# Attention in visits on four 64x64 tiles of TensorE, with a re-timed emission and another load order

## The chip, the cores and the metric

The kernel runs on one core of a Trainium2 chip. Its engines are TensorE (PE; its weight loads are shown apart as PEld), VectorE (DVE), ScalarE (ACT), GpSimd (POOL) and SyncE (SP). The metric is the device time of one execution in microseconds (us); the kernel before has a median of 285.37 us over three runs (285.2 to 285.39).

## The reference

Eight batches of eight heads, 576 positions, head size 64. Retention in parallel form, then a feed-forward with exact GELU:

```python
scores = scale * np.matmul(q, k.transpose(0, 1, 3, 2))
gamma = 1.0 - 2.0 ** (-5.0 - np.arange(H, dtype=np.float32))
Dmat = np.where(rel >= 0, gamma[:, None, None] ** rel[None, :, :], 0.0)   # rel = pos[:, None] - pos[None, :]
attn = np.matmul(scores * Dmat[None, :, :, :], v)
x = attn.transpose(0, 2, 1, 3).reshape(B * S, H * D)      # 4608 x 512
h = x @ w_in                                              # 512 x 2048
g = 0.5 * h * (1.0 + erf(h * inv_sqrt2))
out = g @ w_out                                           # 2048 x 512
```

## The kernel before

**Attention.** The 576 positions are cut into chunks of 128 with a tail of 64, and two batches are worked on together as a pair. A unit is one chunk of one batch (indices 0 to 35; a tail unit holds the tails of both batches of a pair). For a pair of units four things stand on PE: `scores` (k against q, line 535, `sc`), `inner` (values against the masked scores, line 600, `o_ps`), `state` (the decayed sum of k times v that the next chunk reads, line 619, `u_ps`), and `cross` (the state of the chunks before against q, line 653, into the same `o_ps`; a first chunk has none). VectorE masks the scores (`ret`, line 558) and takes `o_ps` out into the rows of x (`xT`); the values are scaled per head into `vh`, in one instruction on DVE or in eight on ACT. The scores of one pair are emitted beside the inner products of the pair ahead of it, so the step that stands together on PE is: inner, state, scores, cross, with small differences of order.

How these use the array of 128 by 128: `inner` and `state` contract over 128 rows and write 64 partitions of the result, so two halves of the columns work side by side. `scores` and `cross` contract over 64 rows and write 64 partitions, so four quarters work side by side. The feed-forward uses the whole array.

**Feed-forward.** Nine blocks of 512 rows of x. `hT` (line 701) is x times w_in, `g` its GELU on ACT, and `oT` (block 0) or seven products with sums of blocks (`m`, line 885; a Strassen form in 2 by 2) give the output. From block 6 the first product is in that form too (`f`, line 966).

**What sets the order.** The program is written by an emission loop that keeps a clock for each engine, with costs and due times written in the code, and at each step emits what its clocks call ready; attention has the first right, then the feed-forward. PE costs are the first argument of `pe(...)`, costs on other engines that of `on(...)`. The table `ORDER` first lists the loads on the POOL queue in order (`wi3` is columns 768 to 1023 of w_in, `k1` the keys of unit 1, `io` the constants, `wo0` rows 0 to 255 of w_out, `dq2` a step of the decay table), then settings: `a7` scales the values of unit 7 on ACT, `s`, `b`, `z`, `p` and `u` delay single steps. In the first 16 us of its clock the loop fills PE's gaps with products of zeros (`warm`). Eight PSUM banks are shared by all products, one bank a result.

```python
if nB < nA:                      # pairs whose scores are there and whose inner products are due
    ...
    cand(max(scored, free_time(n) - 0.3), "S", g, back)
...
elif kind == "S":
    g, back = a
    for i in back:
        inner(i)
```

## Time and profile before

| what | value |
|---|---|
| median of three runs | 285.37 us |
| span of the profiled execution | 283.7 us |
| PE busy | 278.0 us (98%) |
| DVE, ACT, POOL busy | 199.7, 158.8, 114.0 us |
| matrix products on PE | 3361 |

The profile is one execution. A row of the timeline gives the start of a stretch of equal instructions, the time to the end of the last of them, the engine, the line, what is written and read, the shape and the count; a bracket gives idle time ahead of it and what ended it. The products are pipelined, so the time that a stretch really takes is the distance from its start to the start of the next one.

### The profile page before, as it was taken

Reading aid. Unit: us, or ns where it says so; the run is one execution under the profiler, and the core shown is the slowest. Engines: PE = TensorE matmul, PEld = TensorE weight load, DVE = VectorE, ACT = ScalarE, POOL = GpSimd, SP = SyncE. Lnnn points to the kernel's source line nnn. Section 1 sums busy time; section 2 is a strip of 40 time slices with the busy share of each in tenths; the row PEclk is TensorE's granted clock in tenths of the full one; section 3 lists DMA queues with packets and bytes.
Section 4 is the critical chain, followed back from the end, with each engine's and each line's share of the span. In section 5 each row is a group of like instructions: output and inputs, shape, how many; then the busy total and the mean of one; then the engine's idle time right before and its main releaser. Section 6 shows DMA issues by size and latency. Waiting matters only on the chain.

```text
span 283.7 us, 8075 instructions
## 1 busy us (share of the span) xinstructions
PE 278.0 (98%) x3361; PEld 207.6 (73%) x3361; DVE 199.7 (70%) x412; ACT 158.8 (56%) x362; POOL 114.0 (40%) x143
## 2 busy tenths in 40 slices
PE   8989999999999999999999999999999999999994
PEld 3577666688874588548855778558888888888894
DVE  5753483979865595898178867889669968966822
ACT  5676724755456635693298874564565374665320
POOL 8979987993364465625468552000000000000000
PEclk9999999999999999999999999999999999999999
DMA  9999999999999999999999999910003000400133
GB/s 150 165 182 173 188 180 163 146 142 147 172 161 195 190 147 128 156 229 149 135 197 203 147 137 150 222 21 2 0 2 128 23 2 0 151 0 2 74 114 111
DMA packets 152804, 35.39 MB, mean 125 GB/s; under 512 B 141120, under 2 KB 148928, under 8 KB 152768
## 3 DMA queue, kind: packets, MB, share of 16 engines
q0 software_dynamic: 116832, 18.10, 95.3%
q1 hardware_dynamic: 34528, 16.26, 32.9%
q10 hardware_dynamic: 1408, 0.52, 0.7%
q8 instruction: 26, 0.43, 0.7%
q14 instruction: 10, 0.08, 0.1%
HBM read 36.70 MB, written 9.44 MB: 163 GB/s over the span
## 4 chain that ended last, share of the span: by engine, by line
PE 92%; POOL 3%; DMA 3%; issue 0%; DVE 0%; POOLq 0%
PE m L885 35%; PE hT L701 29%; PE f L966 13%; PE oT L746 5%; PE o_ps L600 3%; PE sc L535 3%; DMA w_in<-in_moe_w_in_dram 3%; POOL qk L318 2%; PE o_ps L653 1%; PE u_ps L619 1%; PE qk_ps L482 1%; POOL v_ld L318 1%; POOL w_in L291 1%; PE sc L525 0%; PE o_ps L591 0%
## 5 line engine op out<-in xcount | busy, mean ns | idle before, releaser
L701 PE MATMUL hT<-xT,w_in 128*128 128x512 bf16 (+3 forms) x560 | 87.4, 312 | 0.8 <-DMA w_in<-in_moe_w_in_dram 0.8
L710 ACT ACTIVATE g<-hT 128x512 bf16<-128x512 f32 (+2 forms) x106 | 57.7, 556 | 36.9 <-PE hT L701 36.1
L701 PEld LDWEIGHTS <-w_in 128*128 128x128 bf16 x560 | 48.4, 98 | 33.8 <-DMA w_in<-in_moe_w_in_dram 1.0
L885 PEld LDWEIGHTS <-gs 128*128 128x128 bf16 x656 | 62.2, 98 | 7.7
L885 PE MATMUL m<-w_sum,gs 128*128 128x256 bf16 (+1 forms) x400 | 47.7, 268 | 0.0
L318 POOL DMA_DIRECT2D v_ld<-in_v_dram x40 | 34.0, 854 | 19.3 <-DMA qk_ld<-in_k_dram 8.8
L318 POOL DMA_DIRECT2D qk_ld<-in_k_dram x36 | 30.4, 851 | 21.7 <-DMA qk_ld<-in_q_dram 19.1
L558 DVE TENSOR_TENSOR ret<-sc,msk 128x512 bf16<-128x512 f32 x48 | 30.2, 683 | 12.2 <-PE sc L535 12.2
L318 POOL DMA_DIRECT2D qk_ld<-in_q_dram x36 | 30.4, 851 | 16.9 <-DMA qkT<-qk_ld 6.5
L885 PE MATMUL m<-w_out,gs 128*128 128x256 bf16 x256 | 32.5, 273 | 0.0
L885 PE MATMUL m<-w_sum,g 128*128 128x256 bf16 x256 | 30.9, 273 | 0.0
L572 ACT ACTIVATE vh<-v_ld,dv 128x64 bf16<-128x64 bf16 x120 | 30.0, 339 | 0.0
L782 DVE TENSOR_TENSOR gs<-g 128x1024 bf16<-128x1024 bf16 x32 | 21.8, 686 | 9.0 <-ACT g L710 8.2
L885 PEld LDWEIGHTS <-g 128*128 128x128 bf16 x256 | 24.9, 98 | 3.9
L991 ACT ACTIVATE g<-f 128x512 bf16<-128x512 f32 x36 | 20.2, 590 | 8.9 <-PE f L966 7.5
L786 DVE TENSOR_TENSOR gs<-g 128x1024 bf16<-128x1024 bf16 x32 | 21.6, 684 | 0.0
L672 DVE TENSOR_TENSOR xT<-o_ps,dqT 128x512 bf16<-128x512 f32 (+1 forms) x32 | 18.4, 617 | 4.5 <-PE o_ps L653 4.4
L966 PEld LDWEIGHTS <-w_in 128*128 128x128 bf16 x192 | 18.8, 98 | 2.2
L461 ACT CAST u_sb<-u_ps 128x512 bf16<-128x512 f32 x15 | 8.7, 587 | 16.0 <-PE u_ps L619 16.0
L461 ACT COPY o<-m 128x512 f32<-128x512 f32 x14 | 8.2, 587 | 15.7 <-PE m L885 15.7
L987 ACT ACTIVATE g<-p 128x512 bf16<-128x512 f32 x12 | 7.6, 630 | 14.1 <-DVE p L985 14.1
L966 PEld LDWEIGHTS <-wi 128*128 128x128 bf16 x144 | 14.0, 98 | 1.6
(96 smaller groups left out, 337.6 us busy)
## 6 DMA issues: line engine op xcount, KB each, us to landing
out_dram<-o SPq DMA_DIRECT2D x27, 256.0 KB, 6.3
v_ld<-in_v_dram POOLq DMA_DIRECT2D x32, 128.0 KB, 9.1
qk_ld<-in_k_dram POOLq DMA_DIRECT2D x28, 128.0 KB, 10.7
qk_ld<-in_q_dram POOLq DMA_DIRECT2D x28, 128.0 KB, 8.6
w_in<-in_moe_w_in_dram POOLq DMA_DIRECT2D x8, 256.0 KB, 7.3
w_out<-in_moe_w_out_dram POOLq DMA_DIRECT2D x8, 256.0 KB, 8.0
out_dram<-o SPq DMA_DIRECT2D x14, 128.0 KB, 2.1
qk_ld<-in_q_dram POOLq DMA_DIRECT2D x8, 64.0 KB, 11.4
```

Of the source, the lines that this page charges most:

```text
L318: nc.gpsimd.dma_start(dst, src[2 * bp + jj, :, ci * C:ci * C + n, :].rearrange("h s d -> s h d"))
L461: nc.scalar.copy(dst, src)
L558: nc.vector.tensor_tensor(r, t, by, op=ALU.mult)
L572: nc.scalar.activation(vh[:, h, :], loaded[i][1][:, h, :], AF.Copy, scale=dv[:, h, ci:ci + 1])
L672: nc.vector.tensor_tensor(x_of(i)[:, :, n * x:n * x + n], o, dqT[:, :, ci * C:ci * C + n], op=ALU.mult)
L701: nc.tensor.matmul(hT[:, m, :], lhsT=w[:, cc, o:o + 128], rhs=x_tiles[t][:, cc, lo:hi], start=(cc == 0), stop=(cc == N_DM - 1))
L710: nc.scalar.activation(g_of(t, m0 // 2)[:, m0 % 2:m0 % 2 + n, lo:hi], hT, AF.Gelu)
L782: nc.vector.tensor_tensor(s.rearrange("p m a b -> p m (a b)"), g[:, :, 0, :], g[:, :, 1, :], op=ALU.add)
L786: nc.vector.tensor_tensor(s, g[:, :, :, LEFT], g[:, :, :, RIGHT], op=MINUS)
L885: nc.tensor.matmul(m[:, 0 if apart else ts, :], lhsT=a, rhs=w[:, c0:c1], start=p in begins and mm == 0 and ts == 0, stop=mm == N_DF // 2 - ...
L966: nc.tensor.matmul(m[:, y, :], lhsT=a[:, c], rhs=d[:, c], start=p in (P1, P7) and y == 0 and c == 0, stop=c == 1, skip_group_check=True)
L991: nc.scalar.activation(g[:, :, rows, cols], m, AF.Gelu)
```

## The change

There are three parts.

1. A new function `visit` emits inner, state, scores and cross of a pair as one piece on four 64x64 tiles. Products that contracted over 128 rows are cut into two halves of 64 rows, one on each half of the array's rows, so inner and state have 32 products in place of 16. Of a pair the visit has 32 inner, 32 state, 32 scores and, but for a first chunk, 16 cross. The list has three parts; the second half of each sum over rows stands in the last, behind a wait of PE on a product of its own from the start of the middle part. `whole` says where a visit is taken: when the next pair's scores and all inputs are there by the emission's clock.
2. Costs in the emission are replaced by others (`sum_w` 1.26 for 1.05, the eight scalings on ACT 2.7 for 2.0, products of the tail 0.15 for 0.23, state 0.24 for 0.26, cross 0.2 or 0.12 for 0.23).
3. `ORDER` is another table: among the loads, k, q and v of units 0 to 2 stand ahead of all but two tiles of w_in, and the settings differ. Two units' values are scaled on ACT (`a6`, `a17`) in place of fifteen.

```diff
--- before.py
+++ after.py
@@ -76,6 +76,7 @@
     AHEAD = 14
     A_TURNS = 2
     HOT = 5.3
+    BOTH = 1.1
     N_WARM = 10
     HOLD = 9
 
@@ -193,7 +194,7 @@
         nc.vector.tensor_tensor(s[:, 1], b12, b22, op=MINUS)
         nc.vector.tensor_tensor(s[:, 2], b21, b11, op=MINUS)
         nc.vector.tensor_tensor(s[:, 3:5], w[:, :, 0:256], w[:, :, 256:512], op=ALU.add)
-        ws_at[i] = on("dve", 1.05, land_out[i]) + SEM
+        ws_at[i] = on("dve", 1.26, land_out[i]) + SEM
 
     SW_LATE, HW_LATE = 4.2, 2.8
     TURN_SHARES, STORE_SHARES = (0.455, 0.545), (0.455, 0.545)
@@ -327,15 +328,14 @@
             land[what, i] = (4.6, 5.2)[n] + 0.75 * x
             t = tiles_of(i)
             cast_due[what, i] = (t[1] if what == "v" else t[0][:, "qk".index(what)], first[what, i])
-    ORDER = ("wi1 k1 wi0 io q1 v0 q2 k2 v1 wi2 v2 k3 wi3 q3 v3 wi4 wi5 wi6 k4 q5 k5 q4 v5 wi7 wo1 wo0 k6 v4 dq2 "
...
+    ORDER = ("k1 wi1 io q1 k2 wi0 q2 v0 k3 v1 q3 v2 wi2 wi3 v3 k4 wi4 wi5 q5 dq2 k5 q4 wi7 wi6 v4 wo0 wo1 v6 v5 "
...
 
     BY_ACT = {int(x[1:]) for x in ORDER if x[0] == "a"}
     S_LATE = {int(x[1:].split("+")[0]): float(x.split("+")[1]) for x in ORDER if x[0] == "s"}
@@ -570,7 +570,7 @@
         if by_act:
             for h in range(H):
                 nc.scalar.activation(vh[:, h, :], loaded[i][1][:, h, :], AF.Copy, scale=dv[:, h, ci:ci + 1])
-            st[i]["V"] = on("act", 2.0, at) + SEM
+            st[i]["V"] = on("act", 2.7, at) + SEM
         else:
             nc.vector.tensor_tensor(vh, loaded[i][1], dv[:, :, ci:ci + 1].to_broadcast([128, H, D]), op=ALU.mult)
             st[i]["V"] = on("dve", 0.685, at) + SEM
@@ -590,7 +590,7 @@
                     sl, e = slice(64 * jj, 64 * jj + 64), 64 * (h % 2)
                     nc.tensor.matmul(s["o"][jj][1][e:e + 64, h // 2, :], lhsT=s["vh"][sl, h, :], rhs=s["ret"][0][sl, h, :],
                                      start=(h < 2), stop=False, skip_group_check=True)
-            s["B"] = pe(0.23, 2 * H, "quad")
+            s["B"] = pe(0.15, 2 * H, "quad")
         else:
             s["o"] = [bank([128, HP, 128], FP32, "o_ps")]
             o = s["o"][0][1]
@@ -606,6 +606,99 @@
         elif j == 1 and ci < NCI - 1 and (bp, ci) != (1, 0):
             u_due.append((bp, ci))
 
+    HALF = [slice(0, 64), slice(64, 128)]
+
+    def weave(lists):
+        at, last = [0] * len(lists), None
+        while any(lists):
+            x = min((x for x in range(len(lists)) if lists[x]), key=lambda x: at[x])
+            cols, fn, a = lists[x].pop(0)
+            at[x] += cols
+            last = fn(*a)
+        return last
+
+    def whole(g, back):
+        if len(g) != 2 or len(back) != 2 or back[0] < 4 or units[back[0]][2] != 0:
+            return False
+        bp, ci, _ = units[back[0]]
+        if (bp, ci) == (1, 0) or back != pair_of.get((bp, ci)) or nX != back[0]:
+            return False
+        if ci and u_ready.get((bp, ci - 1), 1e9) > T["pe"] + 0.3:
+            return False
+        if bp and ci == 1 and nX <= units.index((bp - 1, NCI - 1, None)):
+            return False
+        return max(max(st[i].get("V", 1e9), st[i]["R"]) for i in back) <= T["pe"] + 0.3
+
+    def visit(n, bp, ci):
+        pair, g = pair_of[bp, ci], groups[n]
+        if ci == 0:
+            u_bank[bp] = bank([128, H, D], FP32, "u_ps")
+        u_ps, qkT = u_bank[bp][1], sg[n]["qkT"]
+        qT = sg[group_of[pair[0]]]["qkT"]
+        u = u_of(bp, ci - 1) if ci else None
+        at = max(st[i][x] for i in pair for x in "RV")
+        pe_waits(max(at, sg[n]["T"], u_ready[bp, ci - 1] if ci else 0.0))
+        for i in pair:
+            st[i]["o"] = [bank([128, HP, 128], FP32, "o_ps")]
+        got = [[bank([128, HP, 128], FP32, "sc") for _ in range(2)] for _ in g]
+
+        def inner_mm(j, r, e, hp, first):
+            s = st[pair[j]]
+            vals = loaded[pair[j]][1] if pair[j] in raw else s["vh"]
+            return nc.tensor.matmul(s["o"][0][1][HALF[e], hp, :], lhsT=vals[HALF[r], 2 * hp + e, :],
+                                    rhs=s["ret"][e][HALF[r], hp, :], start=first, stop=(not first and hp == HP - 1),
+                                    skip_group_check=True)
+
+        def cross_mm(j, e, hp):
+            return nc.tensor.matmul(st[pair[j]]["o"][0][1][HALF[e], hp, :], lhsT=u[HALF[j], 2 * hp + e, :],
+                                    rhs=qT[HALF[j], 0, 2 * hp + e, :], start=False, stop=False, skip_group_check=True)
+
+        def state_mm(j, r, h):
+            return nc.tensor.matmul(u_ps[HALF[j], h, :], lhsT=loaded[pair[j]][0][HALF[r], 1, h, j, :],
+                                    rhs=st[pair[j]]["vh"][HALF[r], h, :], start=(ci == 0 and h == 0 and j == r), stop=(h == H - 1),
+                                    skip_group_check=True)
+
+        def score_mm(j, c, h):
+            return nc.tensor.matmul(got[j][h % 2][1][HALF[c], h // 2, :], lhsT=qkT[HALF[j], 1, h, HALF[c]],
+                                    rhs=qkT[HALF[j], 0, h, :], start=(h < 2), stop=True, skip_group_check=True)
+
+        tiles = [(r, c) for r in range(2) for c in range(2)]
+        parts = [[[] for _ in tiles] for _ in range(3)]
+        for x, (r, c) in enumerate(tiles):
+            one, mid, two = (part[x] for part in parts)
+            one += [(128, inner_mm, (r, r, c, hp, hp == 0)) for hp in range(HP)]
+            two += [(128, inner_mm, (1 - r, r, c, hp, False)) for hp in range(HP)]
+            (one if r == c else two).extend((64, state_mm, (c, r, h)) for h in range(H))
+            if ci:
+                one += [(128, cross_mm, (r, c, hp)) for hp in range(HP)]
+            (two if r == c else one).extend((128, score_mm, (r, c, h)) for h in (range(4, 8) if r == c else range(4)))
+            mid += [(128, score_mm, (r, c, h)) for h in (range(4) if r == c else range(4, 8))]
+        weave(parts[0])
+        _, fn, a = parts[1][0].pop(0)
+        end = fn(*a)
+        weave(parts[1])
+        tc.add_manual_dep(nc.tensor.nop().ins, end.ins.name,
+                          mybir.DependencyInfo(mybir.DependencyClass.Sync, mybir.DependencyReason.DATA), reason="row tiles")
+        weave(parts[2])
+        done = pe(BOTH + (0.23 if ci else 0.0), 12 * H + 2 * H * (ci > 0), "quad")
+        nonlocal nA, nB, nX
+        nA, nB, nX = nA + 2, nB + 2, nX + 2
+        for j, i in enumerate(g):
+            st[i]["sc"] = got[j], done
+        for i in pair:
+            st[i]["B"], st[i]["Bdone"] = done, True
+        u_ready[bp, ci] = either(0.68, done, u_of(bp, ci), u_ps) + SEM
+        if ci == NCI - 2:
+            release(u_bank[bp][0], u_ready[bp, ci])
+        for i in pair:
+            s_done.add(i)
+        if next_load[0] < len(groups):
+            reload()
+        masked(g[0])
+        for i in pair:
+            evacuate(i)
+        masked(g[1])
+
     def state(bp, ci):
         pair = pair_of[bp, ci]
         assert (bp, ci) == (1, 0) or nX > (pair_of[bp, ci - 1] if ci else pair_of[bp - 1, NCI - 2] if bp else [-1])[-1]
@@ -618,7 +711,7 @@
                 keys = loaded[i][0][:, 1, h, :] if i < 4 else loaded[i][0][:, 1, h, j, :]
                 nc.tensor.matmul(u_ps[64 * j:64 * j + 64, h, :], lhsT=keys, rhs=st[i]["vh"][:, h, :],
                                  start=(ci == 0 and h == 0), stop=(h == H - 1), skip_group_check=True)
-        done = pe(0.26, 2 * H, "col")
+        done = pe(0.24, 2 * H, "col")
         u_ready[bp, ci] = either(0.68, done, u_of(bp, ci), u_ps) + SEM
         u_due.remove((bp, ci))
         if ci == NCI - 2:
@@ -652,7 +745,7 @@
                     sl = slice(64 * j, 64 * j + 64)
                     nc.tensor.matmul(o[64 * e:64 * e + 64, hp, :], lhsT=u[sl, 2 * hp + e, :], rhs=qT[sl, 0, 2 * hp + e, cols],
                                      start=False, stop=(hp == HP - 1), skip_group_check=True)
-        done = pe(0.23, 2 * H, "quad")
+        done = pe(0.2 if j0 is not None else 0.12, 2 * H, "quad")
         for i in g:
             st[i]["B"] = done
 
@@ -1263,6 +1356,11 @@
                 state(*a)
             elif kind == "S":
                 g, back = a
+                if whole(g, back):
+                    visit(group_of[g[0]], *units[back[0]][:2])
+                    while u_due and state_at(*u_due[0]) <= T["pe"] + 0.3 * (nA >= 8):
+                        state(*u_due[0])
+                    continue
                 for i in back:
                     inner(i)
                     nB += 1
```

How it moves the work, at three places. First the POOL queue at the program's start, before and after (`qk_134`, `qk_162`, `qk_225` before and `qk_132`, `qk_148`, `qk_185` after are q and k of units 1, 2 and 3; `w_in_...` one of the eight tiles of w_in, in the order of issue; unit 0's q and k come on other queues):

```order
L291 DMA w_in_132<-in_moe_w_in_dram 128x4x256
L318 DMA qk_134<-in_k_dram 128x8x64
L291 DMA w_in_137<-in_moe_w_in_dram 128x4x256
L143 ISA
L143 IOTA val 128x128
L145 IOTA pos 128x5
L318 DMA qk_134<-in_q_dram 128x8x64
L318 DMA v_ld<-in_v_dram 128x8x64
L318 DMA qk_162<-in_q_dram 128x8x64
L318 DMA qk_162<-in_k_dram 128x8x64
L318 DMA v_ld<-in_v_dram 128x8x64
L291 DMA w_in_196<-in_moe_w_in_dram 128x4x256
```

There the first values (`v_ld`) are the fifth load and the third tile of w_in the ninth. After the change the same queue, from its third load on:

```order
L319 DMA qk_132<-in_q_dram 128x8x64
L319 DMA qk_148<-in_k_dram 128x8x64
L292 DMA w_in_162<-in_moe_w_in_dram 128x4x256
L319 DMA qk_148<-in_q_dram 128x8x64
L319 DMA v_ld<-in_v_dram 128x8x64
L319 DMA qk_185<-in_k_dram 128x8x64
L319 DMA v_ld<-in_v_dram 128x8x64
L319 DMA qk_185<-in_q_dram 128x8x64
L319 DMA v_ld<-in_v_dram 128x8x64
L292 DMA w_in_255<-in_moe_w_in_dram 128x4x256
L292 DMA w_in_265<-in_moe_w_in_dram 128x4x256
L319 DMA v_ld<-in_v_dram 128x8x64
```

Ahead of this piece stand only k of unit 1, one tile of w_in and the constants. The first values move from the fifth load to the seventh, the third tile of w_in from the ninth to the twelfth, and the fourth to the place right behind it.

Second, PE inside a visit, the middle part's end and the last part's start (each product is a weight load and a matmul; `vh` are scaled values, `ret_...` masked scores):

```order
L662 LDWEIGHTS qkT
L662 MATMUL sc<-qkT 64x128
L662 LDWEIGHTS qkT
L662 MATMUL sc<-qkT 64x128
L648 LDWEIGHTS vh [waits PE_49]
L648 MATMUL o_ps<-ret_1790,vh 64x128
L648 LDWEIGHTS vh
L648 MATMUL o_ps<-ret_1792,vh 64x128
```

The last row of scores of the middle part is followed by the second halves of the inner products. Before, on PE too, a pair's inner products stand as one stretch, and the state follows them:

```order
L600 LDWEIGHTS vh
L600 MATMUL o_ps<-ret_2880,vh 64x128
L600 LDWEIGHTS vh
L600 MATMUL o_ps<-ret_2882,vh 64x128
L619 LDWEIGHTS qk_ld [waits DMASW0_49]
L619 MATMUL u_ps<-vh,qk_ld 64x64
L619 LDWEIGHTS qk_ld [waits DMASW1_49]
L619 MATMUL u_ps<-vh,qk_ld 64x64
```

So the scores of the next pair now stand between two halves of the inner products, and the weight load that opens the last part waits for PE itself.

Third, the whole list of PE: a visit is taken seven times, five times with cross and twice at a first chunk, all of them behind the first products on the line of `m` and ahead of the first on that of `f`; the other pairs keep their old form.

2 lines of the change are left out of this document (1 added, 1 removed), and 13 rows, old and new, of the table ORDER.

## The prediction

> **What bounds the kernel now.** I read the page's busy shares and chain first, then PE's waits, then busy time by stage.
>
> ```profile
> PE 278.0 (98%) x3361; PEld 207.6 (73%) x3361; DVE 199.7 (70%) x412; ACT 158.8 (56%) x362; POOL 114.0 (40%) x143
> PE 92%; POOL 3%; DMA 3%; issue 0%; DVE 0%; POOLq 0%
> PE warm L1187 <- DVE zeros L118: 1.2, 1, 1.2
> PE hT L701 <- DMA w_in<-in_moe_w_in_dram: 0.8, 1, 0.8
> 0.00:18.50 18.50, 16.53 (x170) 9.36 (x171) 11.72 (x42) 12.30 (x33) 16.50 (x25) 1.00 1.70 162
> 33.00:75.00 42.00, 42.00 (x581) 30.50 (x580) 33.50 (x79) 21.90 (x51) 32.01 (x40) 1.00 2.08 161
> 75.00:192.00 117.00, 117.00 (x1519) 78.33 (x1518) 85.55 (x167) 72.28 (x182) 52.57 (x64) 1.00 1.79 159
> 192.00:263.00 71.00, 71.00 (x728) 63.09 (x727) 55.51 (x98) 39.13 (x71) 0.00 (x0) 1.00 0.09 31
> ```
>
> The stage rows give length, then busy time of PE, PEld, DVE, ACT and POOL. PE is the bound in the plain sense: the chain is PE for 92%, and PE's whole list of waits has two entries, both in the first 19 us. From 33 to 263 us it is never empty. So nothing can be gained there by ending a wait; the time falls only if PE's own stretches get shorter, or if the start holds fewer warm-up products and waits. It rises if a wait appears where none is now.
>
> **The step that the visit replaces.** These are a step with cross, a first chunk's step, and two pieces that show single rates.
>
> ```profile
> 150.55 0.64 PE L600 MATMUL o_ps<-ret,vh 128*64 128x128 bf16 x16
> 151.02 0.42 PE L619 MATMUL u_ps<-vh,qk_ld 128*64 128x64 bf16 x16
> 151.37 0.64 PE L535 MATMUL sc<-qkT 64*64 64x128 bf16 x32
> 151.84 0.39 PE L653 MATMUL o_ps<-qkT,u_sb 64*64 64x128 bf16 x16
> 152.16 1.04 PE L701 MATMUL hT<-xT,w_in 128*128 128x512 bf16 x4
> ...
> 118.70 0.64 PE L600 MATMUL o_ps<-ret,v_ld 128*64 128x128 bf16 x16
> 119.52 0.64 PE L535 MATMUL sc<-qkT 64*64 64x128 bf16 x32
> 120.09 1.25 PE L701 MATMUL hT<-xT,w_in 128*128 128x512 bf16 x5
> ...
> 110.41 0.32 PE L591 MATMUL o_ps<-ret,vh 64*64 64x64 bf16 x16
> 110.56 0.62 PE L535 MATMUL sc<-qkT 64*64 64x128 bf16 x32
> 111.01 0.29 PE L653 MATMUL o_ps<-qkT,u_sb 64*64 64x64 bf16 x16
> 111.23 0.94 PE L885 MATMUL m<-w_sum,gs 128*128 128x256 bf16 x7
> ```
>
> By distance of starts, the step with cross takes 152.16 - 150.55 = 1.61 us, and the first chunk's 120.09 - 118.70 = 1.39. The same 32 scores take 0.57 when the whole array follows them (119.52 to 120.09) and 0.47 when cross follows (151.37 to 151.84): a change of the array's form costs 0.10. A step before has three such changes: into the halves, from halves to quarters, and back to the whole. A visit has two. The one into it is paid ahead of the first start in both forms, so I leave it out.
>
> On quarters, a product of 128 columns takes between (0.32 - 0.10)/16 = 13.8 ns (cross, 151.84 to 152.16, less the change) and 0.45/32 = 14.1 ns (scores, 110.56 to 111.01). One of 64 columns takes between (0.22 - 0.10)/16 = 7.5 ns (111.01 to 111.23) and 0.15/16 = 9.4 ns (110.41 to 110.56).
>
> A visit with cross has 32 + 32 + 16 = 80 products of 128 columns and 32 of 64. That is 80 x 13.8 + 32 x 7.5 = 1.34 us, or at the upper rates 80 x 14.1 + 32 x 9.4 = 1.43. So the doubled number of products is nearly free: each keeps a quarter of the array busy, where one of the old form kept half. I take 1.34, because a visit is one stretch and the upper rates are of stretches that start anew.
>
> **The new wait inside a visit.** The last part's first weight load waits for a product of PE itself. No row shows PE waiting for PE at close quarters. The nearest rows are a mask that follows scores, and the weight load of a quarter.
>
> ```profile
> 21.24 0.40 PE L516 MATMUL sc<-qkT 64*128 64x128 bf16 x8
> 21.57 2.73 PE L701 MATMUL hT<-xT,w_in 128*128 128x128 bf16 x21
> 21.67 1.29 DVE L558 TENSOR_TENSOR ret<-sc,near 128x512 bf16<-128x512 f32 x2 [1.13 <-PE sc L516]
> L591 PEld LDWEIGHTS <-vh x64: 102/108/110, 73.4 to 225.4; 64*64 64x64 bf16 x64
> ```
>
> Eight scores stand 0.041 us apart. The first mask reads the bank of the seventh, which starts at 21.49, and the mask starts at 21.67: 0.18 from a product's start to whoever waits for it. With the weight load behind it, 0.11, the next product could start 0.29 after the product waited for. Behind that one stand fifteen more scores, 15 x 13.8 = 0.21. What shows is 0.08; the bounds are 0 (the weight load overlaps) and 0.29 (the cover fails). What is queued behind this wait is all of PE, so whatever shows is lost in full.
>
> A visit is then 1.34 + 0.08 + 0.10 = 1.52 against 1.61. A first chunk's has 64 products of 128 columns: 0.88 + 0.24 + 0.18 = 1.30 against 1.39. Both save 0.09, over seven visits 0.63. The ends: 0.17 a visit saved with no wait (1.2 in all); 1.43 + 0.29 + 0.10 = 1.82, 0.21 lost a visit (1.5 in all).
>
> Outside visits the products are the same, but for hT cut into fewer pieces, whose columns are the same. Counting changes of form along both lists from the first oT on gives 53 against 61: seven belong to the visits, one is left: 0.10 saved.
>
> **The values scaled on DVE.** Thirteen units move from ACT to DVE.
>
> ```profile
> L572 ACT ACTIVATE vh<-v_ld,dv x120: 332/337/372, 13.8 to 172.2; 128x64 bf16<-128x64 bf16 x120
> L575 DVE TENSOR_TENSOR vh<-v_ld,dv x21: 680/682/1052, 14.0 to 224.2; 128x512 bf16<-128x512 bf16 x21
> ```
>
> DVE gets 13 x 0.68 = 8.9 us, ACT loses 13 x 8 x 0.337 = 35. I cost this at nothing, because between 75 and 192 us DVE is busy for 85.55 of 117 and has 31 us free. With no cover, a visit would wait one such instruction, 0.68. The other new costs only change what the emission believes; what they do is in the orders already counted.
>
> **The start.**
>
> ```profile
> L1180 PE MATMUL warm<-zeros 128*128 128x512 bf16 x23 | 6.0, 382 | 0.0
> 17.07 0.62 PE L701 MATMUL hT<-xT,w_in 128*128 128x128 bf16 x8
> 18.47 1.05 PE L701 MATMUL hT<-xT,w_in 128*128 128x256 bf16 x8 [0.78 <-DMA w_in<-in_moe_w_in_dram]
> ...
> 11.04 7.39 DMA w_in<-in_moe_w_in_dram
> 1.25 0.88 POOL w_in L291
> ```
>
> In both orders the same products stand ahead of the first oT, so the start differs by warm-ups and waits alone. Before, 23 warm-ups (behind the first ten) are 23 x 0.22 = 5.1 us, and 18.47 - 17.07 less 8 x 0.056 of work is 0.95 of waiting (the row's bracket counts 0.78 of it, the rest lies in modelled ends): 6.0. After, 22 warm-ups are 4.8. The values of unit 0 now come two loads later, 2 x 0.88 = 1.8 us at the queue's pace, and the first hT with them; that is what the warm-ups cover. Behind them the list is work without warm-ups that needs v1, q3, v2 and the third tile of w_in in turn, each about as early as it lands. That tile is issued about 1.25 + 11 x 0.86 + 0.36 for the constants = 11.1 us, when the fourth was before, the one that needed 7.39 us. It would be there at 18.4 if it is hit in the same way, and PE, some 0.3 us later than before at this place, would wait 0.6. I take 0.9 for all waits of the start together: 4.8 + 0.9 = 5.7, 0.3 saved. The ends are no wait (1.2 saved) and 2.1 us of waits (0.9 lost): the hit of 1.4 on a load that PE stands waiting for, and 0.7 for v1 to v2.
>
> **The sum.** 0.63 + 0.10 + 0.3 = 1.0 us off 283.7, a span of 282.7. The profiled execution's span lies 1.7 under the median of 285.37, so I forecast 284.4.
>
> **The rivals.**
>
> *Nothing to measure.* The visit's wait shows in full or the upper rates hold, and the start gains nothing: a visit at 1.61, only the 0.10 is left, 285.3. For it: no row has a PE wait of this kind. Against: the fifteen scores are there as cover.
>
> *The start gets worse.* The whole 0.9 is lost at v0 to w_in: 285.37 - 0.73 + 0.9 = 285.5, still within the measurement. Against: loads of equal size have gone out by the fourth tile in both orders.
>
> *Slower: banks after a visit.* Before, scores end ahead of cross and DVE may begin on them; a visit's results all end with it.
>
> ```profile
> 151.36 0.69 DVE L786 TENSOR_TENSOR gs<-g 128x1024 bf16<-128x1024 bf16 x1
> 152.00 1.29 DVE L558 TENSOR_TENSOR ret<-sc,msk 128x512 bf16<-128x512 f32 x2
> 153.20 1.28 DVE L672 TENSOR_TENSOR xT<-o_ps,dqT 128x512 bf16<-128x512 f32 x2
> 154.40 1.28 DVE L558 TENSOR_TENSOR ret<-sc,msk 128x512 bf16<-128x512 f32 x2
> 152.23 5.29 PE hT L701 x24
> ```
>
> After a step, six of the eight banks wait for DVE. The first comes free 0.18 + 0.64 = 0.82 after the visit's end, if DVE is idle. The second hT needs one at 0.10 + 4 x 0.22 = 0.98. The margin is 0.16, and here DVE came from a `gs` of 0.69. If such an instruction lies in the way, PE waits 0.5: over seven visits 3.5, less 1.0, 287.9. The sign turns at 0.15 a visit. Against: two `hT` in a row do not follow all visits, and before, with DVE as late as 152.00, PE did not wait.
>
> *Slower: the two halves of the state take turns.* In a visit, quarters on different rows write `u_ps` at the same time, one bank, in different partitions; in the rows above, quarters on different rows write different banks (`sc` and `o_ps` have one for each half). Were they to take turns, the 16 state products in each part, 0.25 on two halves before (151.02 to 151.37 less 0.10), take that once more: 0.5 a visit, 3.5 in all, 287.9. The Trainium skill speaks for this one: TensorEngine Tiling (Array Packing), section Restrictions and Gotchas, says that different row tiles cannot access the same PSUM bank simultaneously. No run here shows two row tiles on one bank, so the trace neither agrees nor disagrees; by that rule the sum would be this rival's.
>
> That no visit is taken is ruled out by the order, which has seven.
>
> **How the numbers follow.** The forecast gets 0.52: the span of its own terms, without the worst ends, is 283.2 to 285.2. Nothing to measure gets 0.16, the worse start 0.08, banks 0.18, the state's turns 0.06. This measurement tells apart about 0.2%, 0.57 us: faster is under 284.8, slower over 285.9. So 0.52 faster, 0.24 same, 0.24 slower. The range reaches to 287.0: it leaves out some 0.15 of the two slow rivals' upper half and 0.05 below 283.2.
>
> **What would show it.** A visit's start to the next whole-array product should be 1.52 (first chunk 1.30), with the first product of its last part no more than 0.1 late. PE's list of waits should stay free of DVE and ACT after 33 us. The first oT should start about 0.3 earlier than at 32.79, which is where it starts now:
>
> ```profile
> 32.79 3.63 PE L746 MATMUL oT<-w_out,g 128*128 128x512 bf16 x16
> ```
>
> I am wrong if a visit takes over 1.6, if `sc`, `o_ps` or `hT` waits for DVE behind visits, or if the start is later than now.

## The result, and the profile after

The changed kernel takes 288.05 us (median of 20 runs, 286.36 to 291.07) against 285.48 for the kernel before (median of 20 on the same chip, 285.19 to 287.94). The ratio is 1.0085, with a 95% interval of 1.0064 to 1.0106: slower by about 2.5 us, where 1.0 us less was forecast. The single runs of the changed kernel also lie further apart than those of the kernel before.

The profiled execution ran for 287.86 us, near the median; its span is 286.1 (before 283.7). First its page's busy shares and chain, then the list of PE's waits, then the busy time by stage (length, then PE, PEld, DVE, ACT, POOL, granted clock, DMA share, GB/s).

```profile
PE 277.6 (97%) x3568; PEld 206.6 (72%) x3568; DVE 207.1 (72%) x424; ACT 136.3 (48%) x257; POOL 114.3 (40%) x143
PE 93%; POOL 3%; DMA 2%; issue 1%; DVE 0%; POOLq 0%
```
```profile
PE hT L794 <- issue: 2.2, 2, 2.0
PE warm L1280 <- DVE zeros L119: 1.2, 1, 1.2
PE qk_ps L482 <- ACT qk L461: 0.5, 1, 0.5
PE qk_ps L482 <- DMA qk<-in_q_dram: 0.5, 1, 0.5
```
```profile
33.00:75.00 42.00, 42.00 (x555) 30.64 (x554) 30.94 (x71) 19.20 (x38) 34.30 (x42) 1.00 2.14 161
75.00:192.00 117.00, 114.82 (x1664) 76.51 (x1665) 90.11 (x175) 53.61 (x97) 51.78 (x63) 1.00 1.81 160
192.00:263.00 71.00, 71.00 (x821) 62.75 (x814) 56.72 (x102) 37.57 (x68) 0.00 (x0) 1.00 0.10 32
```

PE was never empty between 33 and 263 us before; now 2.2 us are missing between 75 and 192 (the list's other rows stand in the first 9 us). The wait is for "issue", that is for no engine and no semaphore that the profile shows, and 2.0 of it is at one place. This is the PE timeline there. A row is a stretch of equal products, with its start and the time to the last one's end:

```profile
179.15 0.42 PE L648 MATMUL o_ps<-ret,vh 64*64 64x128 bf16 x16
...
180.91 0.61 PE L794 MATMUL hT<-xT,w_in 128*128 128x512 bf16 x2
183.54 0.81 PE L794 MATMUL hT<-xT,w_in 128*128 128x512 bf16 x3 [2.02 <-issue]
```

Two products of `hT` run from 180.91, the third should follow at 181.34 and starts at 183.54: 2.2 us lost in the middle of a row of equal products. A smaller gap of the same kind, 0.3 at 176 us, makes it 2.5; the visit at 179.15 takes 0.15 longer than the others, with a gap ahead of its first scores. The span grew by 2.4. So in this execution the waits for "issue" are as large as the loss, and everything else together comes out about even.

The visits and the start, in the same timeline:

```profile
32.73 0.59 PE L839 MATMUL oT<-w_out,g 128*128 128x512 bf16 x2
...
123.96 0.42 PE L648 MATMUL o_ps<-ret,v_ld 64*64 64x128 bf16 x16
...
125.33 0.39 PE L794 MATMUL hT<-xT,w_in 128*128 128x512 bf16 x1
...
148.86 0.42 PE L648 MATMUL o_ps<-ret,vh 64*64 64x128 bf16 x16
...
149.56 0.42 PE L662 MATMUL sc<-qkT 64*64 64x128 bf16 x16
149.88 0.42 PE L648 MATMUL o_ps<-ret,vh 64*64 64x128 bf16 x16
...
150.47 0.39 PE L794 MATMUL hT<-xT,w_in 128*128 128x512 bf16 x1
```

A visit takes 150.47 - 148.86 = 1.61 us and a first chunk's 125.33 - 123.96 = 1.37: what the old steps took (1.61 and 1.39). The first oT starts at 32.73, 0.06 earlier than before.

**What the wait for "issue" is.** The page counts the packets of each DMA queue; this row of the changed kernel is the queue that brings the program.

```profile
q8 instruction: 28, 0.46, 0.7%
```

28 transfers of 0.46 MB together are 16.4 KB each. PE's list has 7164 instructions (two for each of 3568 products, and 28 more), which over 28 make 256 each: the program arrives in pieces of 256 instructions. In the trace the packets of one such transfer end at 182.04, and the product at 183.54 is the first of that piece. The Trainium skill says the same of the size (Runtime: NRT & Kernel Launch, section Instruction fetch mechanics: blocks of 16 KiB, 256 instructions, fetched over a DMA queue of the sequencer's own) and adds that the crossing is mostly hidden. The trace agrees on the size; here 2.2 us were not hidden.

### The profile page after: what moved, and what is told of

Same layout as the page of the kernel before. It is cut to its first block, busy times and chain, and to the rows that moved or that the text cites. A ratio compares the mean times of both kernels' runs of the same rounds, so it can differ in the third digit from the quotient of the medians.

```text
span 286.1 us, 8395 instructions
## 1 busy us (share of the span) xinstructions
PE 277.6 (97%) x3568; PEld 206.6 (72%) x3568; DVE 207.1 (72%) x424; ACT 136.3 (48%) x257; POOL 114.3 (40%) x143
## 4 chain that ended last, share of the span: by engine, by line
PE 93%; POOL 3%; DMA 2%; issue 1%; DVE 0%; POOLq 0%
PE m L978 35%; PE hT L794 30%; PE f L1059 13%; PE oT L839 5%; DMA v_ld<-in_v_dram 2%; PE o_ps L600 2%; POOL qk L319 2%; PE o_ps L648 2%; PE sc L535 1%; PE sc L662 1%; PE qk_ps L482 1%; PE o_ps L746 1%; PE u_ps L712 1%; PE u_ps L657 1%; POOL w_in L292 1%
## 5 line engine op out<-in xcount | busy, mean ns | idle before, releaser
L803 ACT ACTIVATE g<-hT 128x512 bf16<-128x512 f32 (+2 forms) x104 | 58.3, 565 | 43.1 <-PE hT L794 42.6
L794 PEld LDWEIGHTS <-w_in 128*128 128x128 bf16 x544 | 47.7, 98 | 36.0 <-issue 3.0
L319 POOL DMA_DIRECT2D qk_ld<-in_q_dram x36 | 30.7, 866 | 18.4 <-DMA qkT<-qk_ld 10.1
L1084 ACT ACTIVATE g<-f 128x512 bf16<-128x512 f32 x36 | 20.2, 590 | 10.5 <-PE f L1059 10.5
L575 DVE TENSOR_TENSOR vh<-v_ld,dv 128x512 bf16<-128x512 bf16 x34 | 22.6, 697 | 1.3 <-DMA v_ld<-in_v_dram 1.2
L1059 PEld LDWEIGHTS <-w_in 128*128 128x128 bf16 x192 | 18.7, 98 | 2.2
L461 ACT CAST u_sb<-u_ps 128x512 bf16<-128x512 f32 x16 | 9.3, 586 | 20.9 <-PE u_ps L657 12.7
L461 ACT COPY o<-m 128x512 f32<-128x512 f32 x13 | 7.6, 586 | 20.1 <-PE m L978 20.1
L1059 PEld LDWEIGHTS <-wi 128*128 128x128 bf16 x144 | 14.1, 98 | 1.7
L839 PE MATMUL oT<-w_out,g 128*128 128x512 bf16 x64 | 14.8, 379 | 0.0
## 6 DMA issues: line engine op xcount, KB each, us to landing
qk_ld<-in_q_dram POOLq DMA_DIRECT2D x8, 64.0 KB, 13.8
```

The costliest lines, as they stand in the source:

```text
L319: nc.gpsimd.dma_start(dst, src[2 * bp + jj, :, ci * C:ci * C + n, :].rearrange("h s d -> s h d"))
L575: nc.vector.tensor_tensor(vh, loaded[i][1], dv[:, :, ci:ci + 1].to_broadcast([128, H, D]), op=ALU.mult)
L794: nc.tensor.matmul(hT[:, m, :], lhsT=w[:, cc, o:o + 128], rhs=x_tiles[t][:, cc, lo:hi], start=(cc == 0), stop=(cc == N_DM - 1))
L803: nc.scalar.activation(g_of(t, m0 // 2)[:, m0 % 2:m0 % 2 + n, lo:hi], hT, AF.Gelu)
L839: nc.tensor.matmul(oT, lhsT=g_of(t, m // 2)[:, m % 2, cols], rhs=w_out_sb[m // 2][:, m % 2, :], start=(m == 0), stop=(m == N_DF - 1))
L1059: nc.tensor.matmul(m[:, y, :], lhsT=a[:, c], rhs=d[:, c], start=p in (P1, P7) and y == 0 and c == 0, stop=c == 1, skip_group_check=True)
```

## The experiments

Each timed run stands beside runs of the kernel before on the same chip (285.3 to 285.6 us). Letters in the expectations: theory A is that PE's program pieces come late; B that the new table costs time by itself; C that the visits do it in another way (in the last two runs with a C, the load order); D and E are explained where they arise. "Lead" is PE's time from 300 instructions ahead of a piece to its first instruction. I take the piece to be asked for there, because in no trace does a piece's transfer start more than 298 instructions ahead of it, and it starts near that where the DMA engines are idle; "slack" is the time from the landing of a transfer to its first user's start.

| run | what | median us | ratio to before, 95% |
|---|---|---|---|
| b_shift48 | before, pieces shifted | 286.70 | 1.0043 [1.0023, 1.0064] |
| e3_shift18 | after, pieces shifted | 287.57 | 1.0052 [1.0029, 1.0074] |
| e2_shift108 | after, pieces shifted further | 289.78 | 1.0154 [1.0114, 1.0194] |
| e1_no_visits | after without visits | 288.77 | 1.0097 [1.0061, 1.0133] |
| f1_stores_held | after, group 16's transposes ahead of stores | 288.85 | 1.0083 [1.0050, 1.0117] |
| f2_store_between | before, a store between them | 285.55 | 0.9978 [0.9950, 1.0007] |
| e5_loads_before | after with the load order of before | 294.13 | 1.0268 [1.0206, 1.0330] |
| e6_loads_after | before with the load order of after | 286.97 | 1.0025 [0.9997, 1.0053] |
| i1_narrow_stores | after, narrow stores | 286.66 | 1.0019 [0.9990, 1.0047] |
| i2_before_narrow_stores | before, narrow stores | 285.30 | 0.9992 [0.9973, 1.0010] |
| i3_no_visits_narrow | no visits, narrow stores | 288.87 | 1.0128 [1.0086, 1.0170] |
| j1c_loads | after, last loads in another order | 289.20 | 1.0120 [1.0071, 1.0168] |
| j4c_loads_narrow | the same and narrow stores | 285.61 | 1.0003 [0.9978, 1.0028] |
| j2c_both | j1c, stores held back | 290.67 | 1.0141 [1.0087, 1.0196] |
| g_after_again | after, one more execution | 288.59 | a single run |

### Is a late piece of the program a cause? (b_shift48, e3_shift18, e2_shift108)

Some of the warm-up products at the start are cut into four (in e2 four or five) narrower ones of the same columns. The work stays the same, but every later instruction moves within its piece, so the pieces begin elsewhere.

```diff
+    cuts_of = [4] * 16            # b_shift48; [4] * 6 in e3, [4] * 20 + [5] * 12 in e2
+    def cut_warm(t):
+        n = cuts_of.pop(0) if cuts_of else 1
+        for x in range(n):
+            lo, hi = 512 * x // n, 512 * (x + 1) // n
+            nc.tensor.matmul(t[:, lo:hi], lhsT=zeros[:, :128], rhs=zeros[:, lo:hi], ...)
```

> The kernel before, which has no visits, its first sixteen warm-up products cut into four, a shift of 48 products (96 instructions) in PE's program. Theory A: the old form too can be hit: PE goes through the pieces that end at 111 and 81 us in 6.8 and 7.3 us, where fetches took about 6 us and 1.5 more: stalls of some tenths to 1 us at one or two places, 285.7 to 287.0 us. If the visits themselves are at fault in another way: 285.4, the same as before.

> The same with only six warm-up products cut into four, a shift of 18 products (36 instructions). Theory A: pieces now end inside or right behind visits three times (141, 173 and 179 us), PE goes through them in 5.9, 6.7 and 7.0 us where the fetches took 5.3 to 9 us and PE went on 1.5 us after a landing: stalls at all three, 289 to 291 us. Theories B and C: 288, no change.

> The changed kernel, same order everywhere, but the warm-up products of the start are cut into four or five narrower ones, so that every later product stands 108 products (216 instructions) later in PE's program at the same time. Theory A: the pieces of the program now begin elsewhere against the visits; the shortest time that PE takes through a piece and its lead behind 141 us grows from 6.9 to 8.9 us by the rows of the changed kernel; the stall behind the visit at 179 us shrinks under 1 us, some small ones may come at 73 to 100 us, where pieces take 7.7 to 8.4 us: 286.0 to 287.0 us. Theories B and C: nothing of it depends on the place in the program, 288 as before the cut.

PE's waits, first in b_shift48, which has no visit at all:

```profile
PE o_ps L653 <- issue: 0.8, 1, 0.8
```

and in e3_shift18:

```profile
PE u_ps L657 <- issue: 1.7, 2, 1.4
PE sc L662 <- issue: 0.4, 1, 0.4
```

In b_shift48 the wait came in one of the two places named beforehand (111 us). In e3 it came in all three foretold places (143, 175 and 183 us), though smaller than foretold: 287.57 where 289 to 291 was expected. By its time alone e3 fits B and C (288) better; what speaks for A are the places of the waits. In the changed kernel and in these three runs the wait stands at the first instruction of a piece each time, though the shifts put the pieces' borders at other products. So the mechanism is shown, and it needs no visit: in b_shift48 old steps stand on the piece's lead. In the places where a PE wait for the program was seen, in any kernel here, PE went on 1.25 to 1.62 us after the piece's last packet (1.99 in one, the 0.3 at 176 us of the changed kernel); where the slack was over 2 us it did not wait.

e2 was a miss for A. Its shortest lead behind 141 us is 8.8 us where the changed kernel has 6.8, and yet it was the slowest of the three, 289.78 where 286 to 287 was expected, mostly for another reason:

```profile
PE sc L662 <- DMA qkT<-qk_ld: 1.5, 1, 1.5
PE qk_ps L482 <- DMA qk<-in_q_dram: 1.3, 2, 0.9
PE sc L535 <- DMA qkT<-qk_ld: 1.1, 1, 1.1
PE u_ps L712 <- issue: 0.7, 1, 0.7
```

PE waits for transposes of q and k (`qkT`), which the kernel before never does after its start. There is a second cause. And a longer lead is no cure by itself: at 83 us PE came to a piece 9.0 us after it was asked for and still waited 0.7, because it had taken 8.2 us to land.

### Are the visits needed for the loss? (e1_no_visits)

```diff
     def whole(g, back):
+        return False
```

> The changed kernel with no visit taken: its own table and costs, but every pair in the old form of inner, state, scores, cross. Theory A (PE runs out of instructions: 16 KB of PE's program, 256 instructions, are fetched at a time, and a visit of 224 instructions in 1.6 us uses them up before the next piece has landed): the stall of 2.2 us behind the visit at 179 us goes, no idle time of PE put down to issue beyond 0.3 us, about 285.4 us, as fast as before. Theory B (the new table's settings or loads cost the time): it stays at 287 to 288.5. Theory C (DVE or banks behind visits): about 285.4 too, but then the stall of the changed kernel should name DVE or ACT.

288.77: without a single visit the table, the costs and the loads cost as much. Theory A alone falls; B comes nearest, and the time is 0.3 above its range. The profiled execution was the fastest of its seven (286.59), without a wait for the program. Its one new wait is late, behind DVE:

```profile
PE f L1060 <- DVE p L1079: 1.3, 1, 1.3
```

It stands at 219 us and is absent from the changed kernel's waits. No run shows whether the values that moved to DVE cause it.

### The order on the SP queue (f1_stores_held, f2_store_between)

In the changed kernel the second transposing load of group 16 stands behind a pair of output stores on the SP queue. POOL's next loads need the buffer that this transpose reads. Longest waits of SP's queue from 126 to 150 us, and of POOL, in the changed kernel; then the POOL row of the kernel before:

```profile
SPq L822 <- DVE o L930: 6.4, 1, 6.4
```
```profile
POOL qk_ld L319 <- DMA qkT<-qk_ld: 10.1, 1, 10.1
```
```profile
POOL qk_ld L318 <- DMA qkT<-qk_ld: 6.5, 1, 6.5
```

Theory D was that these stores set the loads back. f1 holds stores while only one of a group's two transposes is out; f2 puts a pair of stores between the two in the kernel before.

```diff
+    def store(*args):             # f1
+        if nD < len(groups) and len(sg[nD].get("ends", {})) == 1:
+            held_stores.append(args)
+        else:
+            store_now(*args)
```
```diff
+        if nD == 16 and len(sg[nD].get("ends", {})) == 1 and stored[0] <= stored[1]:     # f2, in turnable
+            return None
```

> The changed kernel, with one rule added: no output store is issued while only one of a group's two transposing loads is out. On the SP queue group 16's second transposing load now stands ahead of the pair of stores that it stood behind, as in the kernel before; TensorE's order stays nearly as it was. Theory A (TensorE's program arrives in pieces of 256 instructions, and a piece is waited for where it is asked for shortly before it is needed): the pieces at 144 and 180 us are still tight, so the time stays within 0.3% of the changed kernel's 288. Theory D (a transposing load behind a pair of stores that waits 6.4 us for DVE holds back GpSimd's loads, which then share the DMA queues with everything late in the kernel, instruction pieces too): GpSimd's wait for that transpose falls from 10.1 us to about 6.5, the last groups' transposes land some 3 us earlier against the scores that need them, and the time falls by 1 to 2 us, to 286 to 287.

> The kernel before, with the one pair of output stores of that place put between group 16's two transposing loads on the SP queue; nothing else is meant to move. Theory A: no piece of TensorE's program is asked for later, so 285.4 us, within 0.2% of before. Theory D: GpSimd's wait for that transpose rises from 6.5 us to about 10, its later loads lag by some 3 us, the last groups' transposes land 1 to 4 us ahead of their scores instead of 6 to 9, and the time rises by 0.5 to 2 us, to 286 to 287.5.

D falls. f1's POOL wait went to 7.9 us, and its loads began again at 140.2 us instead of 146.2, but its last load was issued at 182.2 (180.2 in the changed kernel, 173.2 before), and the time is 288.85. f2 is level with the kernel before: its transposes of groups 17 to 20 still landed 5 to 9 us ahead of need. Losing a place in one queue cost nothing where the margins were wide (f2), and winning it back gained nothing in the changed kernel (f1).

### The load order alone (e5_loads_before, e6_loads_after)

```diff
-    ORDER = ("k1 wi1 io q1 k2 wi0 q2 v0 k3 v1 q3 v2 wi2 wi3 ..."
+    ORDER = ("wi1 k1 wi0 io q1 v0 q2 k2 v1 wi2 v2 k3 wi3 q3 ..."     # e5: after with these; e6 the other way
```

> The changed kernel (visits, costs and settings kept) with the order of the first loads of the kernel before. Theory C (the changed load order costs time at the start and in the DMA queues' first 80 us): about 285.5 to 286.5. Theory A: the emission moves with the loads, and the pieces at 83 and 178 us get a lead of only 5.8 and 6.3 us (the changed kernel: 6.9 at the least), so waits of 2 to 3 us on TensorE and 288 to 290.

> The kernel before (no visits, its costs and settings) with the order of the first loads of the changed kernel. Theory C: slower, 286.5 to 288. Theory A: its shortest lead for a piece is 9.4 us against 9.0 in the kernel before, so no wait for the program, and 285.1 to 285.7, with the start's 0.1 us the whole difference.

e6 loses 1.4 us by medians (all twelve runs at 286.7 or more), though its interval just touches 1. Its start is not earlier, and a tile of w_out is late:

```profile
PE oT L738 <- DMA w_out<-in_moe_w_out_dram: 0.6, 1, 0.6
```

e5 was a miss for both theories: 294.13, for a reason that neither named. PE waits 3.2 us for DVE from 84.3 us on. From 85.4 to 92.2 us the granted clock is 0.50, so that the products behind the wait take longer, and the mean of the stage is 0.90:

```profile
PE o_ps L593 <- DVE vh L568: 3.2, 1, 3.2
```
```profile
75.00:110.00 35.00, 30.65 (x455) 19.60 (x456) 23.53 (x42) 14.28 (x29) 18.91 (x23) 0.90 1.81 175
```

Each table's settings did worse with the other's load order. Neither run isolates the order, since the emission writes other queues for other loads.

### Relieving the DMA queues (i1, i2, i3, and the changed kernel once more)

What bounds the loads is seen in the DMA rows from 120 to 192 us (40 slices of 1.8 us; tenths of the time in which the engines were busy), of the kernel before and of the changed one:

```profile
DMA  9999999999999999999999999999999999991000
```
```profile
DMA  9999999999999608999999999999999999999997
```

Before, the engines work without a pause and are done at 186 us. After, there is a hole at 145 us, behind the POOL wait of 10.1, and they work to the end of the stretch. My reading is that engines that are full leave no room to catch up: what is late stays late. It reaches PE in two ways, as transposes and as program. Median time from issue to landing between 172 and 184 us, of the transposes before, after, and with narrow stores (i1):

```profile
qkT<-qk_ld SPq DMA_TRANSPOSE x3, 5.3
```
```profile
qkT<-qk_ld SPq DMA_TRANSPOSE x2, 9.5
```
```profile
qkT<-qk_ld SPq DMA_TRANSPOSE x4, 3.5
```

This is theory E. i1 to i3 store only 32 of the 512 columns of most output tiles, so 15/16 of those bytes stay away from the queues; all instructions and their order stay.

```diff
+            to = hi if t >= N_BLK - 2 else lo + 32
-            queue.dma_start(out[row:row + n, lo:hi], src[p0:p0 + n])
+            queue.dma_start(out[row:row + n, lo:to], src[p0:p0 + n, 0:to - lo])
```

> The changed kernel; of each output tile before the last two blocks only the first 32 of its columns are stored (128 bytes a row in place of 1 or 2 KB), so most of the output is left out; every instruction of TensorE, DVE, ACT and GpSimd and the order of every queue stay. Theory A alone (the pieces are asked for too shortly before they are needed, whatever else the DMA queues do): 287 to 288.5 us, the waits at 176 and 181 us still there. Theory E (the late loads and transposes run behind because the DMA queues are full from 120 to 193 us, and a piece of TensorE's program that is asked for meanwhile takes 8 to 9 us; both then reach TensorE): with 2 MB less to move in that stretch, transposes land earlier, a piece takes 5 us or less there, and the time is 285 to 286, with a smaller spread.

> The same cut in the kernel before: of each output tile before the last two blocks only the first 32 columns are stored, the rest of the output is left out. All theories: its transposes land 6 to 9 us ahead of need and no piece of its program is late, so nothing waits for the stores: 285.4 us, within 0.2%. If it gets faster too, the narrow stores remove something else and the run beside it must be read against this one.

> The changed kernel without visits (as e1_no_visits, 288.8 us), with the same cut of the stores (most of the output left out). Theory E: 285.5 to 287, what is left over 285.4 being TensorE's wait for DVE at 218 us (1.3 us in that kernel's profile). If the loads' lateness was not its cause: 288 to 289.

> The changed kernel once more, another execution: if the program's late pieces are a regular part of its loss, TensorE waits again at product 2518 (181 us) or 1881 (145 us), with a slack near 1.5 us between landing and going on; if its loss moves between causes from execution to execution, other waits (for transposes of late loads) stand in their place.

In i1's profiled execution (span 282.8) the whole list of PE's waits is one row at the start:

```profile
PE warm L1281 <- DVE zeros L119: 1.2, 1, 1.2
```

The piece that was waited for at 181 us took 4.2 us from request to landing, 8.7 in the changed kernel. That is PE's program as it would run with nothing late: 282.8, where the kernel before with the same cut has 283.5 and 282.7 was forecast. But this is the fastest of twelve runs. The median, 286.66, fell by 1.4 only and is above the 285 to 286 that E expected, and the runs go from 284.71 to 288.25: something is left. i2 is unchanged, as expected. i3 did not gain at all, a miss for E as I had it. i3 and the changed kernel's other execution (288.59 us) show a second place. PE's waits in i3, then in that execution:

```profile
PE f L1061 <- DVE p L1080: 1.3, 1, 1.3
PE warm L1282 <- DVE zeros L119: 1.2, 1, 1.2
PE sc L535 <- DMA qkT<-qk_ld: 1.1, 1, 1.1
PE o_ps L747 <- issue: 0.5, 1, 0.5
```
```profile
PE hT L794 <- issue: 1.1, 1, 1.1
PE sc L662 <- DMA qkT<-qk_ld: 0.6, 1, 0.6
PE qk_ps L482 <- DMA qk<-in_q_dram: 0.6, 1, 0.6
PE o_ps L746 <- issue: 0.3, 1, 0.3
PE sc L535 <- DMA qkT<-qk_ld: 0.2, 1, 0.2
```

`sc` at line 535 is group 8's scores (units 11 and 12) at 73 us, and the wait for the program behind it comes at 80 us. Ahead of these scores only two output stores have gone out in i3 (at 67 and 71 us), so narrowing them can help little there. The loss moves between executions: in the first one 2.5 us of program, in this one 1.4 of program and 0.8 of transposes, with 0.3 more at the start. One place returned: the piece that was late at 181 us was late again, by 1.1 us.

### The two places together (j1c, j4c, j2c)

The slack of group 8's and of group 20's last transpose against the first score that reads it, in us, from the trace's landing times and PE's starts:

| kernel | group 8 (73 us) | group 20 (190 us) |
|---|---|---|
| before | 5.1 | 8.9 |
| after, first and second execution | 1.4 / 0.1 | 0.8 / 0.0 |
| f1_stores_held | 0.1 | 0.0 |
| e6_loads_after | 3.7 | 4.1 |
| i1_narrow_stores | 1.0 | 5.3 |
| j1c_loads | 5.7 | 0.0 |
| j4c_loads_narrow | 6.1 | 4.7 |
| j2c_both | 7.1 | 0.0 |

A small slack is no loss yet: before, group 13's transposes land only 1.8 us ahead of need (at 118 us), and PE does not wait.

In the new table k11 and q12, which group 8 needs, are the last two of the ordered loads. The SP timeline from 40 to 90 us begins with the transposes of groups 7 and 8, before and after:

```profile
49.91 11.48 SPq L492 DMA_TRANSPOSE qkT<-qk_ld  x4
```
```profile
52.57 13.45 SPq L492 DMA_TRANSPOSE qkT<-qk_ld  x4
```

j1c moves those loads up. j4c does that with narrow stores. j2c does it with the full output, and holds stores back until the last groups' transposes are out.

```diff
-    "... k8 wo7 q11 v11 q9 q10 k9 k10 v12 v10 k12 dq4 v9 k11 q12 "
+    "... k8 wo7 q11 q9 q10 k9 k10 q12 k11 k12 v9 v10 dq4 v11 v12 "
```
```diff
+        if 17 <= nD < len(groups) or nD == 16 and len(sg[nD].get("ends", {})) == 1:   # j2c, in store
+            held_stores.append(args)
```

> The changed kernel with the last of the ordered loads in another order: k11, q12 and k12, which group 8's transposes need, ahead of v10, v11 and v12. Theory E (two places: group 8's transposes at 73 us, and the late loads at 141 to 193 us): group 8's transposes land 3 to 5 us ahead of its scores (0.0 to 1.4 in the changed kernel), no wait near 73 or 80 us, the second place stays: 286.5 to 287.5 us. If the first place costs nothing in most executions: 288, as the changed kernel.

> The same order of loads, and of each output tile before the last two blocks only the first 32 columns stored (most of the output is left out), so that both places are relieved. Theory E: nothing is left to wait for, 284.6 to 285.2 us with a spread of less than 1.5 us, that is 0.3 to 0.9 us below the kernel before (285.4, and 285.3 with the same cut): the 0.6 to 1.0 us that the visits and the start were predicted to bring. If the visits themselves cost time: 285.5 or more, with no wait in the profile.

> The same order of loads with the full output, and the output stores held back on the SP queue until the transposes of the last groups have been issued (from group 17 on, and between the two of group 16). Theory E: the last groups' transposes land 2 to 4 us earlier than in the changed kernel and TensorE's waits after 140 us shrink: 285.2 to 286.5 us. If the queues are full whatever the order: 287, as with the loads alone.

j1c freed the first place as expected (slack 5.7) and was not faster, a miss in time (289.20 where 286.5 to 287.5 was expected). In its profiled execution the second place cost more, with 2.3 us of waiting at 181 and 193 us, and PE waited 1.6 at the start.

```profile
PE sc L662 <- DMA qkT<-qk_ld: 2.3, 2, 2.0
PE qk_ps L482 <- DMA qk<-in_q_dram: 1.6, 1, 1.6
```

j2c was a miss: with the stores held the transposes of groups 17 to 20 landed later still, and PE waited for three of them (span 291.9 us; the kernel's runs take from 288.77 to 293.89). At the end of the wait of 3.0, from 175.5 us on, the granted clock is 0.50 for 3.4 us.

```profile
PE sc L662 <- DMA qkT<-qk_ld: 6.4, 3, 3.0
```

j4c relieves both places: 285.61, with runs within 2.1 us (284.56 to 286.66) instead of 4.7, and a profiled span of 282.8 again, with no wait after the start. From j1c to j4c, only the stores' bytes differ, and 3.6 us go. So DMA traffic is shown to be the cause of most of the loss. j4c's median is still 0.4 above the upper end of what was expected, and its time is in the range of "the visits themselves cost time". But its visits take 1.60 and 1.37 us, no longer than the old steps, and its profiled span is 0.9 below that of the kernel before. That execution is the fastest of twelve; what the others wait for was not profiled.

No version that computes everything beat the kernel before.

## Why the prediction was wrong

**What failed: the step that prices the new order.** The prediction counted it at the start and at the visits only. Behind the start the loads' new order has no term in the sum, and the new costs stand at nothing ("what they do is in the orders already counted"), because PE's list of waits was empty there. It said that the time rises "if a wait appears where none is now", and then looked for such a wait only inside the visit, at the banks, at the state's halves and at DVE. But the DMA engines were full without a pause up to 186 us, before too, and the transposes' margins (5.1 us for group 8, 8.9 for group 20) stood in no sum. In the changed kernel 1.4 and 0.8 us were left of them, in its second execution 0.1 and nothing. No rival named a transfer after the start, or PE's program. By the runs this is worth some 3.5 us, an estimate: the changed kernel's 288.05, less the 1.7 between span and run time, against the undisturbed 282.8. Of it 1.4 goes with narrow stores alone and 2.4 with the loads' order besides (288.05 to 286.66 and to 285.61); 1.1 stays unexplained. The 287.9 of two rivals is near the measured time by chance: what they describe did not happen.

**The sum for PE's own work came out right by luck.** In the two executions with nothing late the span is 282.8, and 282.7 was forecast, but the terms that make it up are others.

- *Visits, 0.63 forecast: under 0.1 measured* (1.60 or 1.61 against 1.61, 1.37 against 1.39). The mis-sized term is the rate. I took the lower ones (13.8 and 7.5 ns); the upper ones (14.1 and 9.4) hold. The first part has 40 products of 128 columns and 16 of 64: 0.71 by these, 0.70 measured (148.86 to 149.56). The last part is 24 and 16: 0.49, and with the change of form 0.59, as measured (149.88 to 150.47). The argument that one long stretch runs at the lower rates was wrong.
- *The wait inside a visit, 0.08: right.* The middle's sixteen scores take 149.56 to 149.88, 0.32, of which 0.23 is work at 14.1 ns. The scores cover most of it, as argued.
- *The start, 0.3: about right in size, but not steady.* The first oT starts at 32.73 and 33.01 in two executions of the changed kernel, at 32.29 in i1 and at 32.22 in j4c, against 32.79. That goes from a gain of 0.6 to a loss of 0.2. In j1c, which has the same order up to there, it starts at 33.85, a loss of 1.1 where 0.9 was the worst end.
- *From the first oT to the end of the span*, 250.6 in i1 and in j4c against 250.9: nearly 0.4 saved, of which visits and one change of form explain 0.2 at most.
- *DVE's thirteen scalings at nothing: right with the visits.* PE waits for DVE nowhere after 33 us. Without visits it does, 1.3 us at 219 us.

**The signs.** The last part's first product was no more than 0.1 late, and the list of waits stayed free of DVE behind the start. The visit's length, 1.61, passed the limit of 1.6 by a hair, and in the second execution the first oT was later than before, so these two signs did say that the gain would fail. None of the signs looked at a transfer behind the start.

**The rivals.** *Nothing to measure* had the visit right (1.61) and the total wrong. *Banks after a visit* was not seen: no wait of PE for DVE behind any visit. *The state's halves take turns* was not seen either. Both row halves write `u_ps` in the first part, which is no longer than its rates. By the Trainium skill (TensorEngine Tiling (Array Packing), Restrictions and Gotchas) two row tiles may not use one PSUM bank at a time; in time, no such turn shows here, so the measurement decides against that 0.5 a visit.

**What stays open.** Why the DMA engines need longer in the changed kernel late in attention. The rows of the loads' queue from 120 to 192 us, before and after, say that nearly the same number of packets took 9% more time:

```profile
q0 software_dynamic: 35797, 4.50, 110.5%
```
```profile
q0 software_dynamic: 36259, 4.56, 120.4%
```

In f1 that share was 110.9% and the loads were late all the same, so it is not the whole of it. It also stays open whether another order of the same loads would let PE's shorter work pay; with the full output two others were tried (e5, j1c), and neither did.

## What to carry to other kernels

An empty list of waits on the bounding engine says that nothing is late, not that nothing is near: before a change of order, write down for each transfer how long before its use it lands, and look in the DMA row for slices that are not full. Where there are none, only those margins can take up an earlier use or a later issue, and what they cannot take up may show at another place than the one that was changed. And a wait for "issue" on an engine that has all its operands may be its own program: look where its pieces of 256 instructions begin, and whether a dense run of small instructions stands just ahead.

## What the runs showed of the hardware that was not expected

- PE's program comes in pieces of 256 instructions (16.4 KB), and how long one takes goes with the DMA traffic. Counted from 300 instructions ahead, a piece landed after 2.0 us when the DMA engines had little to do (changed kernel at 195 us), after 4.2 with the stores narrowed (i1 at 177 us), after 8.7 in the changed kernel at 182 us and after up to 10.5 (e2 at 194 us). A PE that waits goes on 1.25 to 1.99 us after the last packet.
- 224 instructions in 1.6 us, as a visit has them (160 in the old step), shorten the lead of a piece. The shortest was 9.4 us before (the piece needed at 161 us) and 6.8 after (at 145 us).
- PE waits of 3.2 us (e5, to 87.5 us) and 3.0 us (j2c, to 175.7 us) went with a granted clock of 0.50, for 6.8 us from 85.4 and for 3.4 us from 175.5. With waits of 2.5 us (j2c at 187 us) and 2.0 (changed kernel, j1c) it stayed at 1.00. Two of the changed kernel's longest runs (290.12 and 290.38 us) have a mean granted clock of 0.991 and 0.994, which may be the same; they were not profiled.
- Four 64x64 tiles ran at 14.1 ns for 128 columns and 9.4 ns for 64, also with products of different kinds mixed (0.70 us for a visit's first part, 0.71 by these rates).
